# Attention and two products on one core: the first batch rearranged (g ahead of later q and k, fewer dummies, a chunk's two pairs transposed together, the third chunk's squares behind the first exponentials, its transposes a pair sooner)

## The chip, the cores and the metric

One core of one Trainium2 chip. The metric is device microseconds (us) of one execution, median of several. All runs quoted are fast, that is, none is over 1.5% above the fastest of its kernel. A profile comes from one execution, so its own span can differ from the median.

## The reference

```python
q_n, k_n = rmsnorm(q, g_q), rmsnorm(k, g_k)        # q, k, v: 8 batches, 12 heads, 448 tokens, 64
attn = softmax(q_n @ k_n.T / 8)
x = (attn @ v) gathered to (8*448, 768)
h = x @ w_in                                        # 768 x 2048
out = (h + sin(alpha*h)**2 / alpha) @ w_out         # 2048 x 768
```

## The kernel before

The batch's 12 heads are six pairs; two pairs make a chunk (`c0`, `c1`, `c2` in the first batch). A chunk is squared, reduced, scaled and transposed, then each pair goes through four key tiles of scores (t = 0, 1, then the previous pair's `attend`, then 3, 2). In later batches the second product of the batch before fills TensorE's gaps. In the first there is nothing to fill with but dummy matmuls on a zero tile (`BUSY`). The parts concerned:

```python
psum = ctx.enter_context(tc.tile_pool(name="ps", bufs=4, space=PSUM))    # 4 slots of 2 banks
def bank_pair(name):
    return psum.tile([P, 2, 512], F32, tag="ps", name=name)
...
def rsqrt(ws=slice(0, 2)):                           # early: the first batch's chunks
    ln = npool.tile([P, 2, 2 * NJ], F32, tag="inv", name="inv")
    inv = bank_pair("inv")[:, :, :2 * NJ] if early else ln
    ...
    nc.scalar.activation(ln[:, ws], st.ms[:, ws, :], ACT.Ln, scale=1.0 / D, bias=eps)
    nc.scalar.activation(inv[:, ws], ln[:, ws], ACT.Exp, scale=-0.5)
...
def scores(pi, t, warm=0):
    sc = bank_pair("sc")
    for _ in range(warm):                            # dummies
        nc.tensor.matmul(sc[:, 0], blank[:, :P], blank, start=True, stop=True)
    ...                                              # two matmuls, then ScalarE's exp
...
for p in range(NP):                                  # first batch
    scores(p, 0, BUSY[2 + p])
    scores(p, 1)
    if p:
        attend(p - 1)
    if p == 0:
        c1.rsqrt()
    scores(p, 3)
    scores(p, 2)
    ...                                              # transposes and next chunks' steps
step_of(NC + 1, 6)()
attend(NP - 1)
first_product(0, beside_h(0))
```

PSUM is the memory that matmuls write their results to. The pool hands a tile one of four PSUM slots; which one is fixed when the program is built. A new tile in a slot waits for the last reader of the old one. "exp(p,t)" below is ScalarE's exponential of pair p, key tile t.

The softmax here doesn't subtract the row's maximum and nothing guards it: scores larger than these inputs give would overflow.

## Time and profile before

| | before |
|---|---|
| median, 3 runs | 470.21 us (469.06 to 471.24) |
| span of the profiled run | 468.6 us |
| first product starts | 52.88 us |
| from there to the end | 415.7 us, TensorE full |
| exp(3,0) to exp(4,0) | 32.72 to 43.13, 10.41 us |

### The profile page before, as it was taken

How to read it: one execution, taken by the hardware profiler on the slowest of the kernel's cores; microseconds unless marked ns; L12 is line 12 of the kernel's file. 1: busy time of each engine (PE TensorE's matmuls, PEld its weight loads, DVE VectorE, ACT ScalarE, POOL GpSimd, SP SyncE). 2: the span in 40 equal slices, each digit the busy share in tenths (PEclk: the TensorE clock that was granted, in tenths of full speed). 3: DMA queues.
4: the chain of work that ended last, by engine and by line, in shares of the span. 5: the costliest groups of instructions: out<-in, count | busy, mean ns of one | idle time of the engine just before them, and what ended most of it. 6: DMA issues, size and time to landing. Idle time of an engine off the chain costs nothing.

```text
span 468.6 us, 7778 instructions
## 1 busy us (share of the span) xinstructions
PE 449.6 (96%) x2963; PEld 213.7 (46%) x2966; DVE 227.1 (48%) x331; ACT 345.4 (74%) x554; POOL 285.1 (61%) x285
## 2 busy tenths in 40 slices
PE   7877899999999999999999999999999999999996
PEld 3332454445544454445544454445544455444563
DVE  3754473554644355454734346454744346224621
ACT  5674788878887678987887678986887688886800
POOL 4963887785677567794677566794777556101400
PEclk9897999999999999999999999999999999999999
DMA  6999992569045950559056860559034650311022
GB/s 236 195 238 244 217 216 61 142 151 181 2 151 153 110 136 2 152 163 198 2 111 191 106 142 1 152 153 197 15 97 129 86 80 2 74 35 35 0 51 84
DMA packets 81157, 54.98 MB, mean 117 GB/s; under 512 B 59856, under 2 KB 77280, under 8 KB 81120
## 3 DMA queue, kind: packets, MB, share of 16 engines
q1 hardware_dynamic: 56208, 40.97, 33.7%
q0 software_dynamic: 23968, 11.81, 20.2%
q10 hardware_dynamic: 944, 1.70, 1.0%
q8 instruction: 23, 0.38, 0.3%
q14 instruction: 14, 0.11, 0.1%
HBM read 45.62 MB, written 11.01 MB: 121 GB/s over the span
## 4 chain that ended last, share of the span: by engine, by line
PE 84%; ACT 6%; DVE 4%; issue 2%; POOL 1%; DMA 1%; DVEq 0%; POOLq 0%
PE hps L326 31%; PE ops L367 26%; PE av L295 16%; PE sc L270 7%; ACT expT L274 2%; DVE ms L201 2%; PE sc L272 1%; POOL s L310 1%; ACT rec L298 1%; PE sc L263 1%; PE ps L173 1%; DMA qk<-in_k_dram 1%; ACT rec L297 1%; DVE osb L372 1%; ACT expT L276 1%
## 5 line engine op out<-in xcount | busy, mean ns | idle before, releaser
L367 PE MATMUL ops<-w_out_sb,g_sb 128*128 128x384 bf16 x896 | 161.5, 327 | 1.0 <-DVE g_sb L315 1.0
L274 ACT ACTIVATE expT<-sc 128x896 bf16<-128x896 f32 x144 | 126.7, 914 | 33.0 <-PE sc L270 31.5
L326 PE MATMUL hps<-xT,w_in_sb 128*128 128x448 bf16 x768 | 146.7, 353 | 0.0
L303 DVE TENSOR_TENSOR xT<-av,rec 64x448 bf16<-64x448 f32 x96 | 59.7, 622 | 118.9 <-ACT rec L298 118.2
L310 POOL TENSOR_TENSOR s<-s 128x448 f32<-128x448 f32 x64 | 59.5, 935 | 94.8 <-ACT s L307 83.2
L367 PEld LDWEIGHTS <-g_sb 128*128 128x128 bf16 x896 | 80.8, 98 | 72.2 <-issue 24.5
L315 DVE SCALAR_TENSOR_TENSOR g_sb<-s,inv_alpha_sb,hps 128x448 bf16<-128x448 f32 x128 | 81.3, 676 | 63.2 <-POOL s L310 63.2
L326 PEld LDWEIGHTS <-w_in_sb 128*128 128x128 bf16 x768 | 74.5, 98 | 70.3 <-issue 1.6
L307 ACT ACTIVATE s<-hps,alpha_sb 128x448 f32<-128x448 f32 x128 | 74.6, 627 | 28.6 <-PE hps L326 26.7
L195 POOL TENSOR_TENSOR sq<-qk 128x896 f32<-128x896 f32 x42 | 70.0, 1682 | 12.4 <-DVE ms L201 12.4
L295 PE MATMUL av<-expT,vb 128*64 128x448 bf16 (+1 forms) x384 | 72.2, 371 | 2.9 <-ACT expT L274 2.6
L295 PE MATMUL av<-expT,ones 128*64 128x448 bf16 (+1 forms) x384 | 68.0, 364 | 0.0
L219 POOL TENSOR_TENSOR qkn<-qk,inv 128x448 bf16<-128x448 f32 x42 | 38.5, 938 | 46.2 <-issue 27.1
L198 POOL TENSOR_TENSOR qk<-qk,gg 128x896 f32<-128x896 f32 x24 | 50.2, 2090 | 1.5 <-ACT gg L148 1.5
L270 PE MATMUL sc<-qkT 64*128 64x448 bf16 x288 | 45.0, 361 | 3.2 <-ACT expT L276 1.8
L372 DVE COPY osb<-ops 128x768 f32<-128x768 f32 (+1 forms) x32 | 27.5, 858 | 42.0 <-PE ops L367 41.7
L201 DVE TENSOR_REDUCE ms<-sq 128x14 f32<-128x896 f32 x42 | 44.5, 1080 | 0.7
L295 PEld LDWEIGHTS <-vb 128*64 128x64 bf16 (+1 forms) x384 | 22.6, 109 | 45.5 <-issue 37.9
L297 ACT ACTIVATE rec<-av 128x448 f32<-128x448 f32 x48 | 26.1, 544 | 21.8 <-PE av L295 20.4
L312 ACT ACTIVATE s<-s 128x448 f32<-128x448 f32 x64 | 37.0, 577 | 2.8
L221 POOL TENSOR_TENSOR qkn<-qk,inv 128x384 bf16<-128x384 f32 x42 | 34.0, 830 | 0.0
L298 ACT ACTIVATE rec<-rec 128x448 f32<-128x448 f32 x48 | 27.7, 577 | 1.5
(52 smaller groups left out, 210.0 us busy)
## 6 DMA issues: line engine op xcount, KB each, us to landing
qk<-in_q_dram SPq DMA_DIRECT2D x24, 448.0 KB, 4.6
qk<-in_k_dram SPq DMA_DIRECT2D x22, 448.0 KB, 5.0
out_dram<-osb SPq DMA_DIRECT2D x45, 192.0 KB, 4.5
vb<-in_v_dram POOLq DMA_DIRECT2D x16, 288.0 KB, 8.2
w_in_sb<-in_moe_w_in_dram POOLq DMA_DIRECT2D x2, 1536.0 KB, 17.7
w_out_sb<-in_moe_w_out_dram POOLq DMA_DIRECT2D x2, 1536.0 KB, 32.7
out_dram<-osb SPq DMA_DIRECT2D x14, 96.0 KB, 4.3
qk<-in_k_dram ACTq DMA_DIRECT2D x2, 448.0 KB, 6.0
```

The source lines that it names most:

```text
L195: nc.gpsimd.tensor_mul(st.sq[w], qk[ci][:, w], qk[ci][:, w])
L198: eng.tensor_mul(qk[ci][:, 0], qk[ci][:, 0], gg.to_broadcast([P, 2 * NJ, D]))
L201: nc.vector.reduce_sum(st.ms[:, w, :], st.sq[w], axis=AX.X)
L270: nc.tensor.matmul(sc[:, hi, :S], kt[r, t * P:(t + 1) * P], qt[r, :], start=True, stop=True)
L274: nc.scalar.activation(expT[pi][:, 2 * t:2 * t + 2, :], sc[:, :, :S], ACT.Exp, scale=SCALE)
L295: nc.tensor.matmul(av[o, bank, :S], lhsT, rhs, start=(t == 0), stop=(t == NT))
L303: nc.vector.tensor_mul(xT[b][r, hp, :], av[r, 0, :S], rec[o, :])
L307: nc.scalar.activation(s1, hps, ACT.Sin, scale=alpha_sb[:, m, :])
L310: nc.gpsimd.tensor_mul(s2, s1, s1)
L315: nc.vector.scalar_tensor_tensor(g_sb[:, m, (b % 2) * S:(b % 2 + 1) * S], s2, inv_alpha_sb[:, m, :], hps, op0=ALU.mult, op1=ALU.add)
L326: nc.tensor.matmul(ps[:, m % 2, :S], w_in_sb[:, kt, m * P:(m + 1) * P], x[:, kt, :], start=(kt == 0), stop=(kt == KT - 1))
L367: nc.tensor.matmul(st["ps"][:, k, :HALF], lhsT, w_out_sb[:, m, half * HALF:(half + 1) * HALF], start=(m == 0), stop=(m == MT - 1))
```

## The change

Its intent is an earlier first exponential and a shorter first batch: g's loads are issued behind the first chunk's q and k but ahead of the next ones, on other queues; fewer dummies stand before the first scores; both pairs of chunk 0 are transposed at once; the second chunk's second square moves behind the transposes of k, and the third chunk's squares behind the first pair's exponentials; the third chunk's transposes and the next batch's preparation come a pair sooner. Core of the diff:

```diff
-    BUSY = (36, 6, 0, 4, 4, 4, 4, 4)
+    BUSY = (20, 8, 0, 4, 4, 4, 4, 4)
-    nc.gpsimd.dma_start(out=g_rows[:, 0], ...)
-    nc.gpsimd.dma_start(out=g_rows[:, 1], ...)
+    nc.sync.dma_start(out=g_rows[:, 0], ...)
+    nc.scalar.dma_start(out=g_rows[:, 1], ...)
...
-    c1.square(0), c1.square(1)
+    c1.square(0)
...
-    c0.pe_transpose((0,), (1,), act=True)
-    keep_busy(BUSY[1], blank)
-    c0.pe_transpose((0,), (0,))
+    c0.pe_transpose((0, 1), (1,), act=True)
+    c1.square(1)
+    c0.pe_transpose((0, 1), (0,))
     spread_alpha()
-    c2.square(0), c2.square(1)
-    c2.fold_g()
...
         if p == 0:
-            c0.pe_transpose((1,))
+            c2.square(0), c2.square(1)
+            c2.fold_g()
...
-        if p == 3:
+        if p == 2:
             c2.pe_transpose((0, 1))
...              # next batch: begin_norm at p = 1, 2 (was 1, 3); steps 3 to 6 one pair sooner
```

## The prediction

> **What bounds the kernel now.** I read the page first (engines, slices), then the chain of waits over the first 72 us, then the same stretch cut into windows, then the timeline of 12 to 53 us. A "pair" is two heads; three chunks of two pairs make a batch; "exp(p,t)" is ScalarE's exponential of pair p, key tile t, issued in the order t = 0, 1, 3, 2.
>
> ```profile
> span 468.6 us, 7778 instructions
> PE   7877899999999999999999999999999999999996
> PEclk9897999999999999999999999999999999999999
> ...
> core 0: us, PE busy (x) PEld busy (x) DVE busy (x) ACT busy (x) POOL busy (x), PEclk, DMA share, GB/s
> 0.00:52.88 52.88, 40.61 (x292) 17.07 (x296) 27.10 (x47) 33.20 (x55) 33.43 (x41) 0.90 1.07 224
> 52.88:71.16 18.28, 18.28 (x98) 9.33 (x100) 9.69 (x15) 14.31 (x24) 15.00 (x15) 1.00 1.21 228
> 120.00:180.00 60.00, 59.88 (x392) 28.87 (x391) 30.21 (x43) 45.67 (x75) 41.07 (x39) 1.00 0.50 108
> ```
>
> From 52.88 us, where the first batch's first product starts, TensorE is full. What happens before 52.88 is the whole subject: no matmul of the products can start until six pairs of attention are through, and whatever the change takes off that prologue comes off the end, as everything behind it is bound by TensorE and only moves. The prologue has only 40.61 of 52.88 us of matmul in it, dummies included, at a mean clock of 0.90. Its chain of waits:
>
> ```profile
> 9.95 3.63 PE ps L173 x16
> 13.57 0.31 PE tp L245 x7
> 13.88 0.97 PE ps L173 x4
> ...
> 19.43 1.58 PE sc L263 x4
> ...
> 32.72 0.93 ACT expT L274
> 33.65 0.04 issue
> 33.69 3.00 PE av L295 x16
> ...
> 38.75 0.93 ACT expT L274
> 39.67 0.04 issue
> 39.72 1.07 PE tp L245 x28
> 40.78 0.33 issue
> 41.11 1.49 PE sc L263 x3
> ...
> 52.88 18.28 PE hps L326 x96
> ```
>
> The reader is to see three kinds of loss: dummy matmuls that stand on the chain (3.63 + 0.97 us before the first scores, 1.58 at 19.43, 1.49 at 41.11); an attend that takes 3.00 us at 33.69 though the same 16 steps take 1.60 at 28.10; and exponentials, transposes and scores taking turns from 38 to 43 us. The windows, cut where the granted clock changes, show the second:
>
> ```profile
> 16.35:19.76 3.41, 1.84 (x24) 1.04 (x21) 2.90 (x5) 3.08 (x6) 3.41 (x5) 1.00 1.31 281
> 19.76:23.16 3.40, 3.40 (x16) 1.02 (x15) 3.40 (x7) 2.04 (x3) 3.39 (x4) 0.50 1.34 211
> 23.16:26.57 3.41, 2.13 (x42) 1.21 (x39) 1.71 (x3) 2.50 (x6) 3.41 (x2) 1.00 1.07 226
> 29.99:33.40 3.41, 1.67 (x10) 0.60 (x9) 1.24 (x2) 2.77 (x5) 0.62 (x1) 1.00 1.06 240
> 33.40:36.82 3.42, 3.13 (x18) 1.29 (x17) 0.00 (x0) 1.15 (x3) 0.00 (x0) 0.50 1.06 245
> 36.82:40.24 3.42, 1.06 (x26) 0.71 (x25) 1.25 (x2) 2.36 (x4) 0.00 (x0) 1.00 1.11 268
> ```
>
> After each window with 1.84 us or less of TensorE the clock is 0.50 for the next one; after 2.13 or more it stays 1.00.
>
> **What the Trainium skill says.** "TensorE: Matmul & The Clock Gate", Part 1: the array's clock is either half or full, judged over a free-running window of 3413 ns. The trace agrees: three stretches at 0.50, each 3.4 us long. Free-running means that the phase may fall elsewhere in another run, so part of what follows is luck. The same page's table of specifications calls ScalarE's queue strictly first in, first out; so a square placed between two exponentials delays the second, and I walk ScalarE in program order. "DMA: Bandwidth & Descriptors", "Issuing engines are not separate DMA queues": all transfers share 16 engines, and another issuing engine saves only issue time; in this trace the two g loads cost GpSimd 0.69 and 0.51 us of issue, before anything needs it.
>
> **The change part by part.** I walked the built program of the changed kernel, engine by engine, with its waits and with durations from the profile before: exp of a full tile 0.82 us apart (0.91 alone), of the last tile 0.44, reciprocal's Ln 0.55 and Exp 0.58, a square 0.89, a reduce 0.97, scaling a chunk on VectorE 2.43, one pair's copy 0.6, two xT multiplies 1.26, warm attend 1.60, two scores to the exp 0.40, four dummies 0.95, 28 transposes 0.9.
>
> *g earlier.* Gain about 0. gg is copied at 9.26 us, right after the last inverse root (9.14 + 0.18); g was there at 7.74 already. The fold still starts at 9.54 and ends at 11.63, so the scaled q is ready at 12.85 as before.
>
> *Fewer dummies, both pairs transposed together.* 8 dummies from 9.95 end at 11.8 instead of 16 at 13.6; k's 14 transposes follow; those of q wait for VectorE (12.85), then 0.6, a 0.4 copy, scores at 13.9, exp(0,0) at 14.3. Before: 16.47. So 2.2 us.
>
> *Third chunk's squares behind pair 0.* exp(0,1) ends at 15.95; the second chunk's reduces end at 16.6, so its inverse root ends at 17.1; exp(0,3), exp(0,2) to 18.4; the two squares, 1.8 us, to 20.2; exp(1,0) and (1,1) to 21.9. Before, exp(1,0) began at 21.55: of the 2.2 us, 0.9 is given back here.
>
> *v takes the place of the removed wait.* attend(0) could start at 18.6, but the second part of v, issued at 12.49, landed 8.1 us later, at 20.6, and GpSimd's issue does not move. So TensorE has about 1.3 us of work in the window 16.35 to 19.76 and, with the phase of the run before, runs at half clock to 23.2: attend(0) ends near 23.4, reciprocal 24.5, exp(1,3) and (1,2) to 25.8, xT and the copies of the next pair 26.4, dummies 25.8 to 26.75, exp(2,0) at 27.15. Before: 27.96, so 0.8 us ahead.
>
> *Pair 2.* exp to 28.8, attend(1) to 28.85, reciprocal to 30.0, exp(2,3), (2,2) to 31.2, the third chunk's transposes between, dummies 31.35 to 32.3, exp(3,0) at 32.7. Before: 32.72. The lead is gone, because the dummies now wait for exp(2,2) and not for exp(2,3).
>
> *Pair 3, where the gain is.* Before, few PSUM slots were free (attend(2) waited for exp(3,0) itself), the clock fell, the third chunk's transposes stood at the end of this pair, and exp(4,0) came at 43.13, 10.4 us after exp(3,0). In the changed program attend(2) has a slot of its own, pair 4's keys are already copied, and the chain is exponentials and reciprocal, 4.1 us, plus the next batch's inverse root, 0.5: exp(4,0) at 37.3. That is 5.8 us.
>
> *Pairs 4 and 5.* The same rhythm: exp(5,0) at 41.9, exp(5,2) ends at 45.95, half of attend(5) behind it 0.9: first product at 46.9. Before: 52.88. The inverse root of the next batch's second chunk now stands ahead of exp(5,0) and needs that chunk's k. Before, its loads were issued at 21.79 and 22.20 and took 10.8 and 16.9 us; now they are issued about 1.8 us sooner. Landing at 37.3 to 39.1, a square of 1.68 and a reduce of 1.08 end at 40.1 to 41.9, against ScalarE's arrival at 41.3: 0 to 0.6 us, say 0.3. Sum: 52.9 - 46.9 - 0.3 = 5.7 us.
>
> **The rivals.** (1) Loss by contention: the prologue is bound by transfers (DMA share 1.07), and weights, the next batch's q and k or its transposes arrive too late for the earlier products. For: the first window's share, 1.07, and 1.21 behind it. Against: w_in landed at 39.4, w_out's first half at 49.5 and is needed at 66. If k of the next batch's second chunk lands as late as before or later, 1 to 2 us more are lost: 466. (2) The clock decides: no cold window hits attend(0), and pairs 0 to 2 keep their lead: 1.1 us more, about 463.4; or the phase puts a cold window into pair 3 or 5 as well, 1.5 us less, about 466. (3) ScalarE becomes the bound all the way and eats everything: then the start at 14.3 is worth nothing and the six pairs take as long as before, 470. Against it: ScalarE is busy in 33.20 of 52.88 us. (4) All bubbles close: ScalarE's six pairs at 4.05 us, roots and squares 3.5, from 14.3 give 42.1 and a gain of 10.8; the v wait and the dummies on the chain speak against it.
>
> **Range and chances.** 470.2 - 5.7 = 464.5 us. The clock's phase and the late k make about 1.5 us each way, an unread wait in the walk another 2: 461.5 to 467.5. Faster by over 2% needs 9.4 us, near rival 4: 0.05. Slower by 2% would need a new wait of 15 us against my walk: 0.02.
>
> **What would show it.** The first exponential near 14.3; ScalarE's two squares between 18.4 and 20.2; attend(0) starting at 20.6 when v lands, with the clock at 0.50 there; exp(2,0) and exp(3,0) hardly earlier than before; exp(4,0) 5 to 6 us earlier; the first product at 46 to 48 with 18.28 us unchanged, and the same distance to the end. It is wrong if the first product starts outside 45 to 50, if the lead is already there at pair 2, or if the first product or the second batch no longer runs full and gives time back.

## More of the kernel before

The prediction shows the main lines. Three more, from the timeline of the kernel before, carry pair 3. Columns: start, length, engine, line, operation, output and inputs, shapes, count; in brackets the idle time just before and what ended it.

```profile
33.69 0.58 PE L295 MATMUL av<-expT,vb 128*64 128x448 bf16 x2 [0.82 <-ACT expT L274]
...
38.35 0.36 PE L270 MATMUL sc<-qkT 64*128 64x448 bf16 x2 [1.36 <-ACT expT L276]
...
39.72 1.07 PE L245 MATMUL tp<-ident,qkn 64*128 64x64 bf16 x28 [1.00 <-ACT expT L274]
```

TensorE, which should run ahead of ScalarE, stops three times in a row for an exponential. None of the three needs that exponential as data: attend(2) uses pair 2's, and scores and transposes use none. They wait for the slot that the exponential reads.

## The result, and the profile after

| | before | changed |
|---|---|---|
| median, 4 runs each | 470.73 us (469.06 to 471.42) | 465.53 us (464.32 to 466.52) |
| ratio | | 0.9894 (95%: 0.9856 to 0.9931) |
| span of the profiled run | 468.6 us | 464.8 us |
| exp(0,0) | 16.47 | 14.44 |
| exp(1,0) | 21.55 | 20.00 |
| exp(2,0) | 27.96 | 28.99 |
| exp(3,0) | 32.72 | 35.32 |
| exp(4,0) | 43.13 | 39.85 |
| first product | 52.88 | 49.13 |
| from there to the end | 415.7 | 415.6 |

A ratio here and below is the mean time of one kernel's fast runs over that of the other's fast runs of the same rounds, so it is not quite the ratio of the medians. The predicted time was 464.5 us in a range of 461.5 to 467.5. The profiled run is the slowest of the four.

The chain of waits of the changed kernel (start, length, what; all us):

```profile
12.70 8.29 DMA vb<-in_v_dram
20.99 0.14 issue
21.13 3.00 PE av L295 x15
...
26.59 1.87 PE sc L263 x4
...
35.46 1.60 PE av L295 x16
...
49.13 18.28 PE hps L326 x96
```

The start of the chain is now v's second load, 8.29 us from its issue to its landing, and attend(0) behind it takes 3.00 us where a warm one takes 1.60. The dummies ahead of pair 2 take 1.87 us instead of 0.95. The windows of the changed kernel, cut where the clock changes, say why (busy time of PE, PEld, DVE, ACT and POOL, then the granted clock, the DMA share and GB/s):

```profile
0.00:49.13 49.13, 37.54 (x281) 15.99 (x282) 26.84 (x47) 33.18 (x56) 35.86 (x43) 0.90 1.02 226
...
16.80:20.21 3.41, 1.10 (x7) 0.20 (x4) 2.96 (x6) 3.38 (x7) 2.31 (x5) 1.00 1.36 268
20.21:23.62 3.41, 2.49 (x16) 1.17 (x18) 1.31 (x2) 1.51 (x2) 3.39 (x3) 0.50 1.29 218
23.62:27.03 3.41, 3.04 (x38) 1.78 (x39) 1.65 (x3) 2.76 (x6) 3.41 (x3) 0.50 1.05 242
27.03:30.45 3.42, 3.42 (x16) 1.00 (x16) 2.93 (x7) 1.46 (x2) 3.42 (x5) 0.50 1.06 242
```

While TensorE waits for v it works 1.10 us of 3.41, and then runs at half clock for three windows, to 30.5 us. That costs the lead: at exp(3,0) this run is 2.6 us behind the one before (about 0.8 of it is the third chunk's transposes, which now stand in pair 2; see below). Then pair 3 takes 4.53 us instead of 10.41, and the end is 3.8 us earlier. Two of the three stops of pair 3 are gone; the same steps in the timeline of the changed kernel:

```profile
35.39 0.38 PE L295 MATMUL av<-expT,vb 128*64 128x448 bf16 x2
...
37.15 0.36 PE L270 MATMUL sc<-qkT 64*128 64x448 bf16 x2
```

The third, of the transposes, stands in pair 2 now (33.13, waiting 1.21 us for exp(2,3)). From the first product on nothing differs: 18.28 us for it in both, and the same distance to the end.

### The profile page after: what moved, and what is told of

Its sections match the earlier page's. It is cut to its first block, busy times and chain, and to the rows that moved or that the text cites. A ratio compares the mean times of both kernels' runs of the same rounds, so it can differ in the third digit from the quotient of the medians.

```text
span 464.8 us, 7755 instructions
## 1 busy us (share of the span) xinstructions
PE 446.5 (96%) x2952; PEld 212.7 (46%) x2952; DVE 226.8 (49%) x331; ACT 345.3 (74%) x555; POOL 284.2 (61%) x283
## 4 chain that ended last, share of the span: by engine, by line
PE 82%; ACT 6%; issue 3%; DVE 3%; DMA 3%; POOL 2%; SPq 0%; DVEq 0%; POOLq 0%
PE hps L326 31%; PE ops L367 26%; PE av L295 16%; PE sc L270 6%; ACT expT L274 2%; DMA vb<-in_v_dram 2%; DVE ms L201 1%; PE sc L272 1%; POOL s L310 1%; ACT rec L297 1%; ACT rec L298 1%; DMA g_rows<-in_g_q_dram 1%; DVE osb L372 1%; PE sc L263 1%; ACT expT L276 1%
## 5 line engine op out<-in xcount | busy, mean ns | idle before, releaser
L367 PEld LDWEIGHTS <-g_sb 128*128 128x128 bf16 x896 | 80.8, 98 | 72.2 <-issue 24.5
L297 ACT ACTIVATE rec<-av 128x448 f32<-128x448 f32 x48 | 26.1, 544 | 22.0 <-PE av L295 20.6
L298 ACT ACTIVATE rec<-rec 128x448 f32<-128x448 f32 x48 | 27.7, 576 | 1.5
## 6 DMA issues: line engine op xcount, KB each, us to landing
w_in_sb<-in_moe_w_in_dram POOLq DMA_DIRECT2D x2, 1536.0 KB, 18.9
```

The source lines that it names most:

```text
L367: nc.tensor.matmul(st["ps"][:, k, :HALF], lhsT, w_out_sb[:, m, half * HALF:(half + 1) * HALF], start=(m == 0), stop=(m == MT - 1))
```

## The experiments

Twelve kernels in three calls of four, each on another chip; all gave correct results. The calls are: the changed kernel again, the two halves, and dummies for v; then squares, v, g and the one-line edit; then the last four. The kernel before ran in each: medians 469.23, 470.64 and 469.30 us. Its 33 runs spread over 4.6 us, 467.45 to 472.05, and the record has the mean granted clock of each: the eight at 0.994 to 0.996 took 467.45 to 467.75 us, the six at 0.984 and 0.985 took 471.16 to 472.05, and the rest lie between in nearly the order of their clock. Most of this spread goes with the clock. The ten runs of the changed kernel all had 0.984 to 0.988 and took 464.32 to 466.52, against 470.01 to 472.05 for the 17 runs of the kernel before in that range. So the gain is there in full at like clock.

### The changed kernel again

> The changed kernel once more, to see how much the phase of the clock window moves it. If the phase matters, this trace has its half-clock stretches elsewhere than 20.2 to 30.5 us, the first product starts 1 to 2 us earlier than the 49.13 of the first trace, and the time over the one before is 0.987 to 0.991. If the phase does not matter, the stretches and the 49.13 come back within 0.3 us.

464.75 us, ratio 0.9911 (0.9877 to 0.9944), the upper end of what was expected. In this profile the half clock lies between 10.8 and 24.5 us, four windows long, and begins before the wait for v. exp(2,0) is at 27.61, exp(3,0) at 33.19, and the chain has

```profile
47.00 18.28 PE hps L326 x96
```

So the same program puts its first product at 49.13 or at 47.00, and the spans, 464.8 and 462.6, differ by just that. The half-clock stretch lies earlier here and is even longer (13.7 us against 10.2); that its position makes the 2 us is argued.

### The loop's half alone

```diff
 # kernel before, with only:
-        if p == 3:
-            c2.pe_transpose((0, 1))
+        if p == 2:
+            c2.pe_transpose((0, 1))      # and the next batch's steps a pair sooner, as in the change
```

> The start of the kernel before; of the change only the reordering inside the pair loop (third chunk transposed at the end of pair 2, next batch's steps a pair sooner). My theory (the gain is made at pair 3): attend(2) no longer waits for exp(3,0), exp(4,0) comes 4.5 to 5 us after exp(3,0) and not 10.4, first product at 47.5 to 49, ratio 0.988 to 0.992: as good as the whole change. Rival (the earlier first exponential is what pays): ratio 0.998 to 1.002.

466.48 us, ratio 0.9938 (0.9905 to 0.9971): better than nothing, short of what was expected. Pair 3 behaved as said, exp(3,0) at 32.00 and exp(4,0) at 36.52, 4.52 us apart. What I had not reckoned with came behind it. Its chain of waits:

```profile
22.24 16.97 DMA qk<-in_k_dram
...
39.34 1.69 POOL sq L195
```

The next batch's k landed at 39.2, and its square, reduce and inverse root now stand in front of exp(5,0), which came at 42.66. ScalarE stands still for it for 1.66 us. That is the prediction's first rival, seen here and in neither profile of the changed kernel (exp(5,0) at 44.20 and 42.08), where this k is issued 2 us sooner, at 20.1.

### The start's half alone

```diff
 # changed kernel, with the loop of before and:
     spread_alpha()
+    c2.square(0), c2.square(1)
+    c2.fold_g()
     c1.reduce(0), c1.reduce(1)
```

> The other half alone: g, fewer dummies, both pairs transposed together, with the third chunk's squares ahead of the exponentials and the loop as before. My theory: the first exponential is up to 2 us earlier than 16.47, attend(0) still waits for v until about 21 us, the two-slot congestion at pair 3 is still there, so ratio 0.997 to 1.003. Rival (the earlier start pays): ratio 0.990 to 0.995.

467.88 us, ratio 0.9968 (0.9937 to 0.9999). The start alone brings little; the ratio is just below the expected 0.997, and above the rival's 0.995. exp(0,0) is at 15.80, exp(1,0) at 19.97, exp(2,0) at 27.46, against 27.96 before. Pair 3 is again slow, from 32.22 to 40.07, 7.85 us, though this run has full clock there. The timeline of this run:

```profile
33.19 0.38 PE L295 MATMUL av<-expT,vb 128*64 128x448 bf16 x2 [0.82 <-ACT expT L274]
36.52 0.36 PE L270 MATMUL sc<-qkT 64*128 64x448 bf16 x2 [1.50 <-ACT expT L276]
37.89 0.88 PE L245 MATMUL tp<-ident,qkn 64*128 64x64 bf16 x28 [1.00 <-ACT expT L274]
```

These are the three stops of the kernel before. So they are not the clock's doing. Nor do they bring the half clock by themselves: the three windows that hold them had 1.63, 1.91 and 2.40 us of TensorE, and the clock stayed full to the end of the work. The second of them:

```profile
33.31:36.72 3.41, 1.91 (x20) 0.90 (x18) 0.64 (x2) 2.19 (x4) 0.00 (x0) 1.00 1.06 241
```

### Dummies while TensorE waits for v

```diff
-        scores(p, 1)
+        scores(p, 1, 12 if p == 1 else 0)
```

> The changed kernel with 12 dummies ahead of scores(1,1), in the time in which TensorE waits for v. If the half clock behind that wait is what ate the early lead (20.2 to 30.5 us in the first trace): no stretch at 0.50 between 20 and 30 us, attend(0) 1.6 us instead of 3.0, first product 2 to 3.5 us earlier than 49.13, ratio to the kernel before 0.981 to 0.986. If the landing of v alone sets the pace and the clock costs nothing: same ratio as the changed kernel within 0.002.

463.67 us, ratio 0.9881 (0.9850 to 0.9913). In the profile the clock is full from 14 us on, exp(2,0) is at 26.48 and the first product at 45.88, 3.25 us earlier than in the changed kernel's first profile and 1.1 earlier than in its second. The mechanism is as expected, but the ratio is not the expected 0.981 to 0.986: the gain in the median is 1.1 us, as the first profile was an unlucky one. The interval overlaps with that of the changed kernel, so the gain is hardly resolved.

### The squares ahead of the exponentials again

```diff
 # changed kernel, with:
     spread_alpha()
+    c2.square(0), c2.square(1)
+    c2.fold_g()
...
         if p == 0:
-            c2.square(0), c2.square(1)
-            c2.fold_g()
             c1.scale(0), c1.scale(1)
```

> The changed kernel with its third part undone: the third chunk's squares ahead of the first exponentials again. My theory (attend(0) waits for v until 21 us, so ScalarE has the time anyway): the first exponential 1.3 us later than 14.4, but exp(1,0) at about 20.0 all the same, first product at 46 to 49 as the phase falls, ratio 0.988 to 0.993, the same as the whole change. Rival (the squares on the way to the first scores cost their 1.8 us): ratio 0.993 to 0.996.

464.21 us, ratio 0.9876 (0.9838 to 0.9915). Undoing the third part of the change costs nothing. exp(0,0) is at 15.75, 1.3 us later; exp(1,0) at 19.92; attend(0) at 20.86 as v allows. The move of the squares only changed the order of work that has to be done before v is there. In this run the late k holds exp(5,0) for 0.49 us.

### v issued earlier

```diff
     spread_g()
+    v_parts = load_v(0)
+    v_parts[0](), v_parts[1]()
     keep_busy(BUSY[1], blank)
     c0.fold_g()
     nc.gpsimd.tensor_copy(gate, qk[1][:, 1, 0, 0:1])
-    v_parts = load_v(0)
-    v_parts[0](), v_parts[1]()
```

> The changed kernel with the two large loads of v issued as soon as g is multiplied, about 6.5 us, and not behind the gate at 11.9. If v's landing is what holds attend(0): v lands before 17, attend(0) starts at about 18.5 instead of 21, TensorE has no gap long enough to lose its clock there, exp(2,0) at 25.5 to 26.5, first product at 44.5 to 46, ratio 0.982 to 0.987. Rival (moving v only delays the second chunk's q and k, or the next batch's k then holds exp(5,0)): the start of the squares at 9.6 us or exp(5,0) slips, ratio 0.988 or more.

462.71 us, ratio 0.9843 (0.9808 to 0.9877), and the six runs within 462.42 to 463.00. attend(0) starts at 18.68, exp(2,0) at 25.61, the first product at 45.34. This is the fastest of all kernels here. Its lead is 2.1 us on the changed kernel with g moved back (next experiment). What is left is the other rival: the chain of this run leads through the next batch's k,

```profile
20.28 16.68 DMA qk<-in_k_dram
```

which lands at 37.0 and holds exp(5,0) until 40.4; ScalarE stands still for it for 0.21 us.

### g back on GpSimd

```diff
-    nc.sync.dma_start(out=g_rows[:, 0], ...)
-    nc.scalar.dma_start(out=g_rows[:, 1], ...)
+    nc.gpsimd.dma_start(out=g_rows[:, 0], ...)
+    nc.gpsimd.dma_start(out=g_rows[:, 1], ...)
```

> The changed kernel with g loaded by GpSimd as before. My theory (g is early enough either way): gg is copied at 9.3 to 9.5 as before, same ratio as the changed kernel, 0.988 to 0.993. Rival (g's move pays): at least 0.5 us worse at the first exponential and in the ratio.

464.83 us, ratio 0.9893 (0.9856 to 0.9930), exp(0,0) at 14.13. The move of g's loads is worth nothing.

### The kernel before, with one PSUM tile less

```diff
-            inv = bank_pair("inv")[:, :, :2 * NJ] if early else ln
+            inv = bank_pair("inv")[:, :, :2 * NJ] if ci < 2 else ln
```

> The kernel before with one change of its own: the third chunk's inverse roots are kept out of PSUM, so that slot is not held through pairs 2 and 3. If two free slots made pair 3 slow: attend(2) no longer waits for exp(3,0), exp(3,0) to exp(4,0) takes 5 to 6.5 us instead of 10.4 (7.9 in the start-only run), first product 2 to 4 us earlier than 52.88, ratio 0.990 to 0.996. If the transposes at the end of pair 3 or the clock made it slow, not the slots: 7.5 us or more, ratio 0.998 to 1.002.

464.32 us, ratio 0.9877 (0.9842 to 0.9912), better than expected: one line in the kernel before is worth as much as the whole change. The six runs lie within 464.00 to 464.45. The first product is at 46.71, and pair 3 takes 5.7 us (by the single records exp(3,0) is at 31.59, right behind exp(2,2), and exp(4,0) at 37.26), with the transposes still at its end. The timeline:

```profile
31.75 0.38 PE L295 MATMUL av<-expT,vb 128*64 128x448 bf16 x2 [0.44 <-ACT expT L274]
...
35.08 0.87 PE L245 MATMUL tp<-ident,qkn 64*128 64x64 bf16 x28 [1.21 <-ACT expT L276]
```

attend(2) now waits for its own data, exp(2,2), which ends at 31.7. The clock helps here too: these runs had 0.994 to 0.996. But the kernel before took 467.45 to 467.75 us at that clock, so about 3.3 us are left that no difference of mean clock explains (an estimate, from runs of different calls).

### The changed kernel, with that tile less too

The same one-line edit on the changed kernel.

> The changed kernel with the third chunk's inverse roots kept out of PSUM too. If the change and the slot fix are the same gain got in two ways: ratio within 0.003 of the changed kernel (0.988 to 0.991). If the change has something of its own that a free slot adds to (pair 2's dummies released by an earlier exponential, so that pair 2 takes 4.2 to 4.8 us and not 5.6): first product at 44.5 to 46, ratio 0.984 to 0.987.

463.25 us, ratio 0.9868 (0.9845 to 0.9890). The second expectation is met in all its numbers: the first product is at 45.75, pair 2 takes 4.77 us, and the ratio lies in its range. What that is worth on top of either alone is not resolved: the interval overlaps with theirs.

### Everything together, with and without dummies

```diff
 # v early, inv out of PSUM for c2, and:
-        if p == 4:
+        if p == 5:
             step_of(NC + 1, 5)()
```

> The changed kernel with v early, the third chunk's inverse roots out of PSUM, and the inverse root of the next batch's second chunk one pair later, so that the late k no longer stands in front of exp(5,0). If these waits are separate: attend(0) at 18.5, pair 2 in 4.2 to 4.8 us, exp(5,0) not held, first product at 42.5 to 44, ratio 0.978 to 0.983. If the waits only take each other's place: not better than v early alone, 0.984.

464.57 us, ratio 0.9898 (0.9876 to 0.9920): worse than v early alone. The first expectation fails; the second, no better than v early alone, holds, but with 0.984 it expected no loss. The run is ahead until exp(2,0), at 24.89, but exp(3,0) comes only at 32.7. VectorE and GpSimd in this run:

```profile
24.88 3.86 DVE L219 TENSOR_TENSOR qkn<-qk,inv 128x448 bf16<-128x448 f32 x2
...
25.62 2.09 POOL L198 TENSOR_TENSOR qk<-qk,gg 128x896 f32<-128x896 f32 x1
```

Two multiplies that took 1.14 us together in the changed kernel take 3.86, until GpSimd's multiply is through at 27.7. With the inverse roots out of PSUM both inputs of VectorE's multiply are in SBUF, the main on-chip memory. In the Trainium skill "SBUF — State Buffer", section "Who interferes with whom", says that such a multiply contends with a GpSimd instruction that reads SBUF, and that the port pair which the two share is an exclusive lock. The runs agree, both ways. With v early alone, where the roots are in PSUM, the same multiplies run beside GpSimd's undisturbed:

```profile
25.36 1.14 DVE L219 TENSOR_TENSOR qkn<-qk,inv 128x448 bf16<-128x448 f32 x2
...
22.83 3.33 POOL L195 TENSOR_TENSOR sq<-qk 128x896 f32<-128x896 f32 x2
```

With the roots in SBUF they take 1.15 us where no GpSimd multiply overlaps (the one-line edit on the kernel before), 1.62 where the end of one does (the edit on the changed kernel), and 3.86 here. The transposes behind them wait until 28.8, and a half-clock stretch from 30.6 to 34.1 adds to the delay.

```diff
-    BUSY = (20, 8, 0, 4, 4, 4, 4, 4)
+    BUSY = (20, 8, 0, 4, 0, 0, 0, 0)
```

> The same without the dummies of pairs 2 to 5. If they only stand on the chain: 0.5 to 1.5 us less than the run with them, no half clock. If they carry the clock: stretches at 0.50 between 24 and 45 us, and 1 to 3 us more than the run with them.

462.93 us, ratio 0.9863 (0.9838 to 0.9888), 1.6 us less than with the dummies: those of pairs 2 to 5 stand on the chain. This run has half-clock stretches from 16.1 to 19.5 and from 29.7 to 33.1 us. The first lies ahead of the dummies that were taken out, the second where the run with them has one too (30.6 to 34.1). So no stretch is seen that comes of their absence; that they carry the clock is not shown.

### Two slots held on purpose

```diff
 # changed kernel, p == 2:
             c2.pe_transpose((0, 1))
+            held = [bank_pair("held") for _ in range(2)]
+            for h in held:
+                nc.tensor.matmul(h[:, 0, :P], blank[:, :P], blank[:, :P], start=True, stop=True)
 # p == 3:
+            for h in held:
+                nc.vector.tensor_copy(gate, h[:, 0, 0:1])
```

> The changed kernel with two of the four PSUM slots held through pair 3 by two tiles that do nothing else: the built program then has attend(2) wait for exp(3,0) and scores(3,2) for exp(3,3), as the kernel before had. If the slots are what the change cured at pair 3: exp(3,0) to exp(4,0) takes 6.5 to 8 us and not 4.5, first product 2 to 4 us later, ratio 0.994 to 1.000. If the earlier transposes alone cured it: 4.5 to 5.2 us, ratio as the changed kernel.

468.05 us, ratio 0.9963 (0.9925 to 1.0001): most of the gain is gone, as expected. exp(3,0) is at 33.25, exp(4,0) at 39.96, 6.71 us, and the stops are back:

```profile
34.22 0.38 PE L295 MATMUL av<-expT,vb 128*64 128x448 bf16 x2 [0.77 <-ACT expT L274]
...
37.54 0.36 PE L270 MATMUL sc<-qkT 64*128 64x448 bf16 x2 [1.50 <-ACT expT L276]
```

Two reservations: the holding tiles also make pair 4's dummies wait for VectorE (0.50 us), and the clock is half from 39.4 to 42.8, which lengthens pair 4 and not pair 3.

The slots that the built programs give pair 3, in program order, beside its length:

| program | scores t0, t1 | attend(2) | scores t3, t2 | transposes here | exp(3,0) to exp(4,0) |
|---|---|---|---|---|---|
| before | 2, 1 | 2 | 1, 1 | 1 | 10.41, half clock twice |
| start only | 2, 3 | 2 | 3, 3 | 3 | 7.85 |
| changed, two slots held | 0, 2 | 0 | 2, 2 | none | 6.71 |
| before, one tile less | 2, 3 | 0 | 2, 3 | 2 | 5.7 |
| changed | 3, 1 | 0 | 2, 3 | none | 4.53 |
| loop only | 1, 0 | 3 | 2, 1 | none | 4.52 |

Where attend shares its slot with t0's scores, it waits for the exponential that reads them; the slow rows have that, the fast ones don't. The slots were not short, they were dealt badly: in the built kernel before, slots 0 and 3 hold the third chunk's inverse roots and attend(1)'s result, whose last readers end at 29.97 and 32.17 us in its trace, and then lie empty until pair 4, while pair 3 takes turns on 1 and 2. Why the pool dealt them so is not shown.

## Why the prediction was right, and where its terms were off

**The time.** 5.7 us were predicted off the end, 5.2 were measured, and the place was right: the gain is made at pair 3, and everything from the first product on only moves.

**g earlier, 0.** Right: putting g back changed nothing.

**Start, 2.2 us to 14.3.** Right: 14.44. So was the walk of ScalarE: squares from 18.32 to 20.1, exp(1,0) at 20.00 against a predicted 20.2. Reading a strictly ordered queue with durations from the profile before was good to 0.2 us here.

**The squares.** The text said that they give back 0.9 us of the start. By the experiment this is not a loss that could be saved: with the squares first, exp(1,0) is as early (19.92), and attend(0) waits for v in any case.

**v takes the place of the wait.** Right: landing at 21.0 against 20.6, and TensorE stopped for it by name. Issuing v earlier brought 2 us.

**The clock behind it.** Here a size was off. The term was "runs at half clock to 23.2", one window. In the first profile it was three windows, to 30.5, so that exp(2,0) came at 28.99 instead of 27.15. The step that failed is the rule I read from the profile before, that a window with 2.13 us of TensorE or more keeps or restores full clock. The window 20.21 to 23.62 had 2.49 us and the next one 3.04, and both restored nothing. 1.49 us of the second were transposes, and the Trainium skill's "TensorE: Matmul & The Clock Gate", Part 4, says that a transpose does not count as busy in the same way; that fits the second window, but the first had no transpose in it. Nor does the rule hold at full clock: with v early a window with 2.25 us lost it. What decides stays open. The second profile of the same program fell otherwise and came to 27.61, 33.19 and 47.00, where the prediction had 27.15, 32.7 and 46.9 (47.2 with its 0.3 for the late k). So rival 2, the clock's phase, fits a difference of about 2 us between two runs, as the range allowed.

**Pair 3, 4.6 us.** Right: 4.53. The prediction named three causes together: few free slots, the clock, the transposes. The experiments part them. These are differences between different runs, so estimates: half clock 10.41 - 7.85 = 2.6 us, slots 7.85 - 5.67 = 2.2, transposes moved away 5.67 - 4.53 = 1.1. The last is mostly given back in pair 2, which takes 5.58 us with the transposes in it (27.61 to 33.19) against 4.76 before. That few slots were free was a misreading: two were empty, and the deal was at fault. The half clock may follow from the stops, since TensorE was idle in them, but need not: the start-only run has the stops at full clock, the kernel before and the run with two slots held have half clock during or behind them. So the change works in good part, and with the half clock mainly, because it makes the pool deal out other slots; that the half clock belongs to this is argued. One line that takes a tile out of the pool does the same.

**The late k, 0.3 us.** It cost nothing in the changed kernel: the inverse root followed exp(4,2) at once. It is real, though: it cost ScalarE 1.66 us in the loop-only kernel, 0.49 with the squares first and 0.21 with v early.

**Open.** Where the half-clock stretches lie in each timed run is not known, as only one execution of each kernel has a trace; the other runs have only their mean clock. What a version with v early, the late inverse root and all scaling kept out of GpSimd's way would reach was not run.

## What to carry to other kernels

When an engine waits for something that it doesn't need as data, look at which buffer slot its output has: the built order and the slots tell more than the source, and reordering steps can deal the slots anew without anyone meaning it. Taking one short-lived tile out of a pool may be worth as much as a rewrite, but see what else is slowed when it goes to another memory. A gain ahead of a load that has not landed is no gain; move the load.

## What the Trainium skill lacked or had wrong

- "TensorE: Matmul & The Clock Gate": the window of 3.4 us and the two clocks are as it says. It lacks how much of a window has to be busy. By the busy time of these profiles there is no clear limit: at full clock a window with 1.91 us kept it (start only, 33.3 to 36.7), one with 2.25 lost it (v early, 13.5 to 16.9); at half clock 2.79 us restored it (start only, 19.7 to 23.1) and 2.83 did not (two slots held, 15.5 to 18.9). Of the four only the one that lost it has transposes in it, 0.25 us.
- The same page calls the ramp's penalty under 1% of a typical kernel. That is not contradicted, but it is no small number here: 2.1 us of 463 lie between two profiles of one program, 0.5%, and 4.6 us, 1%, between runs of the kernel before in the order of their clock, against a change of 5.2.
- "DMA: Bandwidth & Descriptors" says that an engine goes round-robin between software and hardware queues, and gives no figure for it: a load of k that took 4.9 us at the start, beside other loads of q and k and small ones, took 16.7 to 17.0 beside the loads of weights and v from the software queue.
- No page has how a pool's slots are dealt out when the program is built, or how a profile tells a wait for a slot from one for data: attend(2) waiting 0.82 us for an exponential that it does not read.
